# First eight attention blocks of an attention and expert kernel: order written by hand, fourth chunks' weights turned on TensorE

## The chip, the cores and the metric

One core of a Trainium2 chip runs the whole program. The metric is device time in microseconds. The core's engines are TensorE (PE in the profile, with its weight loads as PEld), VectorE (DVE), ScalarE (ACT), GpSimd (POOL) and SyncE (SP, which only issues DMAs here). Each runs its own list of instructions in the listed order and waits at an instruction until what it needs is there.

## What is computed

```python
# attention: q (4, 12288, 128), kv (4, 384, 32, 128), w_sr (128, 128)
kv_pool = kv.reshape(B, H // 4, 4, W // 4, 4, C).mean(axis=(2, 4))
k = v = kv_pool.reshape(B, -1, C) @ w_sr             # 768 keys for each batch
s = (q @ k.transpose(0, 2, 1)) / sqrt(C)
a = exp(s - s.max(-1)); a /= a.sum(-1) + 1e-9
x = (a @ v).reshape(B * N, C)                        # 49152 rows
# experts: w_gate (128, 8), w1 (8, 128, 1024), w2 (8, 1024, 128)
logits = x @ w_gate; e = argmax(logits); p = softmax(logits)[e]
y = p * (maximum(x @ w1[e], 0) @ w2[e])
```

## The kernel before

Rows go in 96 blocks of 512, 24 to a batch; a block has four chunks of 128 rows. Numbers are split in a high and a low half where needed (qh and ql, ah and its low half, xh and xl), so that a product is three matmuls.

**Keys of the first batch.** `kv_load` brings six tiles of raw keys in two halves each; `kv_pool` sums the first half on DVE (`pooled`), and `kv_turn` adds `pooled` and the eight pieces of the second half while turning them, nine matmuls in that order; `kv_turned` copies the result (`pT`), `kv_project` multiplies it with w_sr, `kv_high` and `kv_low` write the key halves `k_sb`.

**A block t of attention.** `q_load` (four DMAs), `q_turn` (DVE, qT), `q_high` (ACT, qh), `q_low` (ql). For each chunk c, `scores` is a generator in steps: six matmuls into a PSUM tile `s`; the row maximum `nmax` (DVE, lines 317 and 318); the exponentials `a` (ACT, line 321); the cast `ah`; the low half `ah` (POOL, line 332) and one DMA that turns both halves into `aT` (line 333). `block_values` multiplies aT with the values two blocks later (18 matmuls), `block_high` and `block_low` make xh and xl, `block_logits` and `block_sum` the gate's logits.

**Experts.** Blocks are grouped (two in the first group, then four); a group's gate (`gate`) finds its most frequent expert, `group_load` fetches that expert's weights, `weight_scales` and `split_expert` scale and split them. Block t - 8 goes through its expert while block t is at its scores (LAG is 8).

**What sets the order.** From block 8 on, a hand-written table of times (`at`, in steps of LEN = 18.7) sets the order of every engine; the times are only keys for sorting, nothing waits for them. The keys of the first batch and blocks 0 to 7 stand in a plain loop ahead of that (`early_scores`, `early_tick`, `early_values`), and the language's scheduler chooses the order on each engine from priorities. In these blocks the cast `ah` of every chunk is on DVE, ql is on DVE, and the DMAs of q are issued from ACT. PSUM holds two `s` tiles and a third (`s2`) for chunk 2, and two other banks (`ps_f`).

Where the text speaks of a step of the table, block t's step begins at t times 18.7, and the lines of that step are `block_scores` at +0, +3.65, +9.25 and +14.85, and `block_values` at +6.0 and +11.6.

## Time and profile before

| | |
|---|---|
| time, median of 3 runs | 1948.69 us (1944.15 to 1950.67) |
| profiled execution | 1945.67 us, of which the span is 1943.9 us |
| TensorE busy | 1877.9 us (97%), mean granted clock 0.989 of full speed |
| DVE, ACT, POOL busy | 1436.2, 1290.3, 1367.6 us |
| chain that ended last | PE 89%, DVE 4%, DMA 3% |

Times in rows are microseconds from the start of the span, unless marked ns. A duration of a matmul holds the way through the array, so matmuls overlap in the rows: the pace of TensorE is the distance between starts. PEclk is the granted clock of TensorE, 1.00 for 2.4 GHz and 0.50 for 1.2 GHz.

### The profile page before, as it was taken

Reading aid. Unit: us, or ns where it says so; the run is one execution under the profiler, and the core shown is the slowest. Engines: PE = TensorE matmul, PEld = TensorE weight load, DVE = VectorE, ACT = ScalarE, POOL = GpSimd, SP = SyncE. Lnnn points to the kernel's source line nnn. Section 1 sums busy time; section 2 is a strip of 40 time slices with the busy share of each in tenths; the row PEclk is TensorE's granted clock in tenths of the full one; section 3 lists DMA queues with packets and bytes.
Section 4 is the critical chain, followed back from the end, with each engine's and each line's share of the span. In section 5 each row is a group of like instructions: output and inputs, shape, how many; then the busy total and the mean of one; then the engine's idle time right before and its main releaser. Section 6 shows DMA issues by size and latency. Waiting matters only on the chain.

```text
span 1943.9 us, 30335 instructions
## 1 busy us (share of the span) xinstructions
PE 1877.9 (97%) x9908; PEld 1095.8 (56%) x9908; DVE 1436.2 (74%) x2800; ACT 1290.3 (66%) x2346; POOL 1367.6 (70%) x1385
## 2 busy tenths in 40 slices
PE   6779999999999999999999999999999999999987
PEld 5555555555555555555555555555555555555444
DVE  6787877778787787766777877867767667677685
ACT  2347667676767767767667667677677677676554
POOL 1567787776878777777688688677677776776353
PEclk9889999999999999999999999999999999999999
DMA  8798888767988876878888887776777777676352
GB/s 193 140 164 174 164 164 177 155 128 156 197 160 166 181 152 130 161 139 147 162 149 187 170 153 143 152 150 139 146 136 147 135 145 142 125 154 134 87 129 46
DMA packets 1012385, 290.61 MB, mean 149 GB/s; under 512 B 916960, under 2 KB 994914, under 8 KB 1012224
## 3 DMA queue, kind: packets, MB, share of 16 engines
q1 hardware_dynamic: 995072, 286.44, 74.5%
q10 hardware_dynamic: 16896, 2.10, 0.7%
q8 instruction: 79, 1.29, 0.3%
q14 instruction: 82, 0.67, 0.1%
q0 software_dynamic: 256, 0.10, 0.0%
HBM read 81.34 MB, written 30.15 MB: 57 GB/s over the span
## 4 chain that ended last, share of the span: by engine, by line
PE 89%; DVE 4%; DMA 3%; issue 1%; ACT 1%; POOL 0%; SPq 0%; ACTq 0%; POOLq 0%; DVEq 0%
PE m L136 44%; PE y L136 24%; PE s L136 21%; DMA aT<-ah 1%; DVE hl L454 1%; DVE nmax L317 1%; DMA kv_raw<-in_kv_dram 1%; DVE ah L326 1%; DMA aT<-in_kv_dram 0%; DVE ws L401 0%; ACT a L321 0%; ACT hh L448 0%; DMA q_sb<-in_q_dram 0%; ACT kv_raw L431 0%; SPq L178 0%
## 5 line engine op out<-in xcount | busy, mean ns | idle before, releaser
L332 POOL TENSOR_TENSOR ah<-a,ah 128x768 f16<-128x768 f32 x388 | 641.4, 1655 | 385.8 <-ACT ah L330 294.3
L448 ACT ACTIVATE hh<-m 128x512 f16<-128x512 f32 (+1 forms) x784 | 463.7, 593 | 411.3 <-PE m L136 408.2
L454 DVE SCALAR_TENSOR_TENSOR hl<-m,hh 128x512 f16<-128x512 f32 (+1 forms) x784 | 533.0, 681 | 228.2 <-ACT hh L448 199.0
L136 PE MATMUL s<-k_sb,qh 128*128 128x384 f32 x1552 | 476.9, 388 | 9.5 <-ACT qh L516 9.0
L321 ACT ACTIVATE a<-s,nmax 128x768 f32<-128x768 f32 x388 | 351.1, 905 | 167.1 <-DVE nmax L318 130.7
L136 PE MATMUL m<-aT,v_sb 128*128 128x512 f16 (+1 forms) x1764 | 413.1, 378 | 15.7 <-DMA aT<-ah 9.8
L317 DVE TENSOR_REDUCE nmax<-s 128x1 f32<-128x768 f32 x388 | 369.3, 953 | 73.2 <-PE s L136 64.9
L136 PEld LDWEIGHTS s<-k_sb,qh 128*128 128x128 f32 x1552 | 293.2, 193 | 68.0 <-ACT qh L516 10.2
L136 PE MATMUL m<-xh,w1h 128*128 128x512 f16 (+1 forms) x776 | 296.3, 382 | 7.5 <-DVE hl L454 6.7
L136 PE MATMUL y<-hh,w2h 128*128 128x512 f16 (+1 forms) x776 | 293.1, 378 | 2.7 <-ACT y L477 1.8
L136 PEld LDWEIGHTS <-v_sb 128*128 128x128 f16 x1764 | 170.9, 98 | 219.8 <-issue 11.7
L136 PE MATMUL m<-xl,w1h 128*128 128x512 f16 (+1 forms) x776 | 293.5, 378 | 0.0
L136 PE MATMUL y<-hh,w2l 128*128 128x512 f16 (+1 forms) x776 | 293.2, 378 | 0.0
L136 PE MATMUL m<-xh,w1l 128*128 128x512 f16 (+1 forms) x776 | 293.2, 378 | 0.0
L136 PE MATMUL y<-hl,w2h 128*128 128x512 f16 (+1 forms) x776 | 293.2, 378 | 0.0
L136 PE MATMUL s<-k_sb,ql 128*128 128x384 f32 x776 | 267.3, 345 | 2.5 <-DVE ql L521 2.4
L136 PEld LDWEIGHTS <-w2h 128*128 128x128 f16 x1552 | 151.6, 98 | 183.5 <-issue 6.2
L136 PEld LDWEIGHTS <-w1h 128*128 128x128 f16 x1552 | 125.0, 101 | 131.0 <-issue 56.2
L328 POOL CAST ah<-a 128x768 f16<-128x768 f32 x178 | 146.8, 824 | 72.2 <-ACT a L321 72.2
L348 DVE SCALAR_TENSOR_TENSOR xl<-m,xs,xh 128x512 f16<-128x512 f32 (+1 forms) x98 | 73.0, 745 | 130.7 <-ACT xh L343 128.6
L483 POOL COPY o<-yT 128x512 uint16<-128x512 uint16 x190 | 137.2, 767 | 22.8 <-DMA yT<-y 22.8
L330 ACT CAST ah<-a 128x768 f16<-128x768 f32 x178 | 148.9, 836 | 3.9 <-DMA aT<-ah 1.6
(211 smaller groups left out, 2037.4 us busy)
## 6 DMA issues: line engine op xcount, KB each, us to landing
kv_raw<-in_moe_w_dram SPq DMA_DIRECT2D x54, 512.0 KB, 4.7
out_dram<-o SPq DMA_DIRECT2D x96, 256.0 KB, 2.2
q_sb<-in_q_dram SPq DMA_DIRECT2D x352, 64.0 KB, 2.5
kv_raw<-in_kv_dram SPq DMA_DIRECT2D x84, 256.0 KB, 4.6
aT<-ah SPq DMA_TRANSPOSE x388, 3.8
aT<-in_kv_dram SPq DMA_DIRECT2D x12, 256.0 KB, 7.5
k_dram<-k_sb SPq DMA_DIRECT2D x8, 384.0 KB, 3.1
q_sb<-in_q_dram ACTq DMA_DIRECT2D x32, 64.0 KB, 3.0
```

The source lines that it names most:

```text
L136: nc.tensor.matmul(o, l, r, start=start, stop=stop)
L317: nc.vector.tensor_reduce(nmax, pss[:, :, :KH], axis=AX.XY, op=ALU.max, negate=True)
L321: nc.scalar.activation(a.rearrange("p (h k) -> p h k", h=2), pss[:, :, :KH], AF.Exp, bias=nmax, scale=1.0, accum_out=sums)
L326: nc.vector.tensor_copy(ah[:, 0], a)
L328: nc.gpsimd.tensor_copy(ah[:, 0], a)
L330: nc.scalar.copy(ah[:, 0], a)
L332: nc.gpsimd.tensor_sub(ah[:, 1], a, ah[:, 0])
L348: nc.vector.scalar_tensor_tensor(xl[:, :n], po[:, :n], k["xs"][:, 0:1], xh[:, :n], op0=ALU.mult, op1=ALU.subtract)
L448: nc.scalar.activation(hh[:, :n], ph[:, :n], AF.Relu)
L454: nc.vector.scalar_tensor_tensor(hl[:, :n], ph[:, :n], 0.0, hh[:, :n], op0=ALU.max, op1=ALU.subtract)
L483: nc.gpsimd.tensor_copy(o.bitcast(U16).rearrange("p c (d i) -> p i c d", i=2)[:, i], yT.rearrange("p (i c) d -> p i c d", i=2)[:, i])
```

## The change

The plain loop of blocks 0 to 7 is gone. `first_keys` and a new table, `plan_short`, write out their order by hand, in steps of SHORT = 9.8; `plan_first` places the first group's gate and its expert's weights in those steps, and `plan_group` has a case of its own for the second group. The table from block 8 on is as before. In the same go:

- `scores` has a second way for a chunk (`by_pe`), taken by chunk 3 of blocks 0 to 6: TensorE turns the exponentials `a` in six 128x128 transposes into two PSUM banks, ACT copies them to aT's high half (two copies of 128x384), DVE subtracts to the low half (two of 128x384). That chunk has no cast, no subtraction on POOL and no DMA.
- The casts of chunks 0 and 2 go from DVE to ACT and those of chunk 1 (and chunk 3 of block 7) to POOL, as they are from block 8 on; ql goes from DVE to POOL, except block 0's.
- PSUM is divided from the start as later: two `s` tiles, three banks m, one bank y. The third `s` tile goes; the values of blocks 0 to 5 go to bank y.
- q's DMAs of blocks 2 to 9 are issued from SP instead of ACT, behind the turning DMAs of the block before; q of block 0 is loaded in front of the last two tiles of keys.
- In a tile of keys the eight pieces of the second half are added first and `pooled` last.
- The four DMAs that keep the first batch's keys for the tail (`kv_keep`) go to the steps of blocks 11 to 14.

```diff
-    early = ExitStack()
-    ps_e = early.enter_context(tc.tile_pool(name="ps_e", bufs=1, space=bass.MemoryType.PSUM))
-    ps_f = early.enter_context(tc.tile_pool(name="ps_f", bufs=2, space=bass.MemoryType.PSUM))
-    EXPERTS = {}
+    EXPERTS = {name: sb.enter_context(tc.tile_pool(name=f"ps_{name}", bufs=1, space=bass.MemoryType.PSUM))
+               for name in "my"}
...
+        if by_pe:
+
+            kts = [slice(lo, lo + KT // 2) for lo in (0, KT // 2)]
+            pts = []
+            for ks in kts:
+                pt = bank()[:, :KH].rearrange("p (t c) -> p t c", c=P)
+                for i, t in enumerate(range(ks.start, ks.stop)):
+                    nc.tensor.transpose(pt[:, i], a[:, t * P:(t + 1) * P], ident)
+                pts.append(pt)
+            yield
+            for ks, pt in zip(kts, pts):
+                nc.scalar.copy(aT[:, ks, cs], pt)
+            yield
+            for ks, pt in zip(kts, pts):
+                nc.vector.tensor_sub(aT[:, KT + ks.start:KT + ks.stop, cs], pt, aT[:, ks, cs])
+            return
         ah = three.tile([P, 2, NK], F16, name="ah")
-        if not EXPERTS:
-            nc.vector.tensor_copy(ah[:, 0], a)
-        elif c % 2:
+        if c % 2:
             nc.gpsimd.tensor_copy(ah[:, 0], a)
         else:
             nc.scalar.copy(ah[:, 0], a)
...
-    raws = {t: kv_load(0, t) for t in range(KT)}
-    for t in range(2):
-        q_load(t, nc.sync)
+    raws = {}
+    for t in range(KT):
+        raws[t] = kv_load(0, t)
+        if t == KT - 3:
+            q_load(0, nc.sync)
+    q_load(1, nc.sync)
...
+    LEN, SHORT = 18.7, 9.8
+    FIRST = LAG * (LEN - SHORT)
...
+    def plan_short(t):
+
+        T, z, y = begin(t), t - 2, t - 3
+        by_pe = t < LAG - 1
+        for c, time in enumerate((0.0, 2.36, 4.72, 7.1)):
+            at(T + time, block_scores, t, c, by_pe and c == 3)
+            at(T + time + 1.1, block_part, t, c)
+            at(T + time + 2.3, block_part, t, c)
+        for c, times in enumerate(((5.76, 6.7), (5.8, 8.4), (8.1, 10.0))):
+            for time in times:
+                at(T + time, block_part, t, c)
...
+        if t > 0:
+            for time in (1.07, 3.42, 4.67):
+                at(T + time, block_part, t - 1, 3)
+        if z >= 0:
+            at(T + 3.43, block_values, z, range(0, 2))
+            at(T + 5.78, block_values, z, range(2, 4))
+            at(T + 8.16, block_values, z, range(4, KT))
+            at(T + SHORT + 0.8, block_high, z)
+            at(T + SHORT + 2.27, block_low, z)
...
+        at(T + 0.2, q_load, t + 2, nc.sync)
+        at(T + (-0.2 if t else 2.31), q_turn, t + 1)
+        at(T + (1.5 if t else 3.4), q_high, t + 1)
+        at(T + (1.95 if t else 3.4), q_low, t + 1, nc.gpsimd)
...
+        if t < LAG:
+
+            T = LAG * LEN
+            group_gate(g)
+            for _ in range(6):
+                at(T + 3.5, gate_part, g)
...
+        first_keys()
+        for t in range(LAG):
+            plan_short(t)
+            run(begin(t + 1) - 0.5)
```

From the end of block 8's step on, PE, DVE, ACT and POOL have the same instructions in the same order in both programs, and SP has too but for the four DMAs of `kv_keep`. What differs ahead of that is shown at three places.

TensorE at the end of the keys; m is the bank of a tile of keys, kv_raw its second half. Before:

```order
L136 MATMUL m<-ident,pooled 128x128
L136 MATMUL m<-ident,kv_raw 128x128 x8
L136 MATMUL m<-pT,wsr 128x128 x2
L136 MATMUL s<-k_sb,qh 128x384 x2
L136 MATMUL s<-k_sb,ql 128x384
```

Now:

```order
L131 MATMUL m_281<-ident,kv_raw 128x128 x8
L131 MATMUL m_290<-pT,wsr 128x128
L131 MATMUL m_281<-ident,pooled 128x128
L131 MATMUL m_299<-pT,wsr 128x128
L131 MATMUL s<-k_sb,qh 128x384 x2
L131 MATMUL s<-k_sb,ql 128x384
```

The eight pieces of the last tile and the projection of the tile before now stand in front of `pooled`.

VectorE in the step of block 3. Before:

```order
L326 CAST ah<-a 128x768
L512 STREAM_TRANSPOSE qT<-q_sb 128x512
L326 CAST ah<-a 128x768
L521 TENSOR_TENSOR ql<-qT,qh 128x512
L317 TENSOR_REDUCE nmax<-s 128x1
L348 SCALAR_TENSOR_TENSOR xl<-m,xs,xh 128x512
L318 TENSOR_SCALAR nmax<-nmax 128x1
L326 CAST ah<-a 128x768
L317 TENSOR_REDUCE nmax<-s 128x1
L326 CAST ah<-a 128x768
L318 TENSOR_SCALAR nmax<-nmax 128x1
L317 TENSOR_REDUCE nmax<-s 128x1
```

Now:

```order
L309 TENSOR_REDUCE nmax<-s 128x1
L310 TENSOR_SCALAR nmax<-nmax 128x1
L354 SCALAR_TENSOR_TENSOR xl<-y,xs,xh 128x512
L309 TENSOR_REDUCE nmax<-s 128x1
L310 TENSOR_SCALAR nmax<-nmax 128x1
L367 TENSOR_REDUCE lg<-m_639 128x32
L330 TENSOR_TENSOR aT<-m_613,aT 128x3x128
L330 TENSOR_TENSOR aT<-m_617,aT 128x3x128
L309 TENSOR_REDUCE nmax<-s 128x1
L310 TENSOR_SCALAR nmax<-nmax 128x1
L309 TENSOR_REDUCE nmax<-s 128x1
L310 TENSOR_SCALAR nmax<-nmax 128x1
```

The four casts and ql have left; the two subtractions of the fourth chunk of the block before have come, and each nmax has its line 310 right behind it.

ScalarE in the same step. Before:

```order
L321 ACTIVATE a,sums<-s_645,nmax 128x768
L343 ACTIVATE xh<-m,xs 128x512
L508 DMA q_sb<-in_q_dram 32x16x32
L321 ACTIVATE a,sums<-s,nmax 128x768
L508 DMA q_sb<-in_q_dram 32x16x32 x3
L321 ACTIVATE a,sums<-s,nmax 128x768 x2
L516 CAST qh<-qT 128x512
```

Now:

```order
L313 ACTIVATE a,sums<-s,nmax 128x768
L327 CAST aT<-m_613 128x3x128
L327 CAST aT<-m_617 128x3x128
L313 ACTIVATE a,sums<-s,nmax 128x768
L336 CAST ah<-a 128x768
L313 ACTIVATE a,sums<-s,nmax 128x768
L336 CAST ah<-a 128x768
L313 ACTIVATE a,sums<-s,nmax 128x768
L349 ACTIVATE xh<-y,xs 128x512
L522 CAST qh<-qT 128x512
```

The four issues of q have left ScalarE; two copies and two casts have come between the exponentials.

## Rows read from the trace of the kernel before

**Rows 1.** Windows: us, busy us (count) of each engine, PEclk, DMA share, GB/s.

```profile
32.60:143.90 111.30, 82.63 (x384) 58.03 (x385) 89.60 (x179) 44.68 (x87) 63.90 (x46) 0.85 0.82 153
...
181.34:368.50 187.16, 187.16 (x994) 108.75 (x992) 143.66 (x258) 129.06 (x240) 150.40 (x160) 1.00 0.84 167
```

**Rows 2.** Waits, 32.5 to 144: waiter, awaited, us in total, times, longest.

```profile
PE m L136 <- DMA aT<-ah: 9.8, 3, 3.7
...
PE s L136 <- ACT qh L516: 9.0, 5, 3.8
```

**Rows 3.** Groups by form, 32.6 to 143.9: busy us, mean ns, idle before.

```profile
L332 POOL TENSOR_TENSOR ah<-a,ah 128x768 f16<-128x768 f32 x32 | 55.9, 1747 | 71.6 <-DVE ah L326 55.4 <-issue 5.9 <-DVE gate L373 3.0
...
L317 DVE TENSOR_REDUCE nmax<-s 128x1 f32<-128x768 f32 x33 | 30.8, 950 | 16.0 <-PE s L136 16.0
...
L321 ACT ACTIVATE a<-s,nmax 128x768 f32<-128x768 f32 x33 | 29.8, 902 | 59.1 <-DVE nmax L318 39.6 <-DVE vst L239 3.8 <-DVE nmax L317 3.5
...
L326 DVE CAST ah<-a 128x768 f16<-128x768 f32 x32 | 27.3, 854 | 3.3 <-DMA aT<-ah 3.1
...
L521 DVE TENSOR_TENSOR ql<-qT,qh 128x512 fp32r<-128x512 f32 x9 | 6.9, 766 | 1.4 <-ACT qh L516 1.4
```

**Rows 4.** Timeline of TensorE, first step of the later table: start, us, instruction.

```profile
132.01 0.62 PE L136 MATMUL s<-k_sb,qh 128*128 128x384 f32 x2 [1.24 <-ACT qh L516]
...
143.86 2.10 PE L136 MATMUL m<-aT,v_sb 128*128 128x512 f16 x9 [0.60 <-DVE hl L454]
...
152.50 0.69 PE L136 MATMUL s<-k_sb,qh 128*128 128x384 f32 x2
```

**Rows 5.** Timeline, end of the keys.

```profile
26.36 1.89 DVE L186 TENSOR_REDUCE pooled<-kv_raw 128x128 f32<-128x1024 f32 x1 [1.64 <-DMA kv_raw<-in_kv_dram]
...
30.50 0.71 DVE L512 STREAM_TRANSPOSE qT<-q_sb 128x512 f32<-128x512 f32 x1 [1.86 <-DMA q_sb<-in_q_dram]
```

**Rows 6.** The same of TensorE.

```profile
28.70 1.95 PE L136 MATMUL m<-ident,kv_raw 128*128 128x128 f32 x16
...
32.60 0.62 PE L136 MATMUL s<-k_sb,qh 128*128 128x384 f32 x2 [1.04 <-ACT qh L516]
```

**Rows 7.** DMA queues and issues, 32.6 to 143.9: packets, MB, share; KB, us to landing.

```profile
q1 hardware_dynamic: 53323, 14.87, 69.8%
q10 hardware_dynamic: 16896, 2.10, 12.0%
...
q_sb<-in_q_dram ACTq DMA_DIRECT2D x31, 64.0 KB, 3.0
...
aT<-ah SPq DMA_TRANSPOSE x32, 4.1
```

**Rows 8.** Timeline of TensorE in a later step, with transposes of 128x128 f32.

```profile
763.12 0.52 PE L136 MATMUL s<-k_sb,qh 128*128 128x384 f32 x2
...
763.66 0.38 PE L272 MATMUL s<-ident,vT 128*128 128x128 f32 x2
763.88 0.38 PE L136 MATMUL m<-xh,w1h 128*128 128x512 f16 x1
```

**Rows 9.** Groups by form, 400 to 1500, as rows 3.

```profile
L454 DVE SCALAR_TENSOR_TENSOR hl<-m,hh 128x512 f16<-128x512 f32 x466 | 319.9, 687 | 135.1 <-ACT hh L448 116.2
...
L330 ACT CAST ah<-a 128x768 f16<-128x768 f32 x116 | 97.1, 837 | 2.7 <-DMA aT<-ah 1.6
L328 POOL CAST ah<-a 128x768 f16<-128x768 f32 x116 | 95.6, 824 | 47.4 <-ACT a L321 47.4
...
L521 POOL TENSOR_TENSOR ql<-qT,qh 128x512 fp32r<-128x512 f32 x58 | 73.7, 1270 | 4.6 <-ACT qh L516 4.5
...
L431 ACT ACTIVATE kv_raw<-kv_raw,ws 128x1024 f32<-128x1024 f32 x31 | 35.6, 1149 | 0.5
```

**Rows 10.** Windows of 1 us, columns as rows 1.

```profile
41.00:42.00 1.00, 0.43 (x2) 0.43 (x3) 1.00 (x2) 0.00 (x0) 1.00 (x1) 1.00 0.14 29
...
43.00:44.00 1.00, 0.99 (x4) 0.48 (x2) 1.00 (x4) 0.37 (x1) 0.50 (x2) 0.50 0.80 150
```

More of the change, by code (lines that the diff above doesn't have):

```diff
@@ L198, in kv_turn @@
         k["pt"] = pt
-        parts = [k.pop(("pooled", t))] + k.pop(("parts", t), [])
+        parts = k.pop(("parts", t), []) + [k.pop(("pooled", t))]
         if len(parts) == 1:
@@ L557, in block_values @@
             if kt == 0:
-                BL[t]["po"] = bank(start, end)
+                BL[t]["po"] = bank(start, end) if start else EXPERTS["y"].tile([P, 512], F32, name="y")
             values(BL[t]["po"], BL[t]["aT"], k, kt, BLK)
@@ L877, in done, with first_keys @@
         return 0 <= t < NBLK
-    raws = {t: kv_load(0, t) for t in range(KT)}
-    for t in range(2):
-        q_load(t, nc.sync)
-    gate_weights()
-    def kv_project_all(b, t):
-        kv_project(b, t, bank()[:, :P])
-        kv_high(b, t)
-        kv_low(b, t)
-    for t in range(KT):
-        kv_pool(0, t, raws.pop(t))
-        kv_turn(0, t, bank()[:, :P])
-        kv_turned(0, t)
-        if t == KT - 1:
-            q_prep(0)
-        if t > 0:
-            kv_project_all(0, t - 1)
-    kv_project_all(0, KT - 1)
+    raws = {}
[4 more added lines that the diff above has]
+    q_load(1, nc.sync)
+    gate_weights()
+    def first_keys():
+        for t in range(KT):
+            kv_pool(0, t, raws.pop(t))
+            pt = bank()[:, :P]
+            k = KEYS[0]
+            own = k.pop(("pooled", t))
+            parts = k.pop(("parts", t))
+            for i, part_ in enumerate(parts):
+                mm(pt, part_, ident, i == 0, False)
+            if t > 0:
+                kv_project(0, t - 1, bank()[:, :P])
+                kv_high(0, t - 1)
+            mm(pt, own, ident, False, True)
+            k["pt"] = pt
+            kv_turned(0, t)
+            if t > 0:
+                kv_low(0, t - 1)
+            if t == KT - 2:
+                q_prep(0)
+        kv_project(0, KT - 1, bank()[:, :P])
+        kv_high(0, KT - 1)
+        kv_low(0, KT - 1)
     extra = [dict(n=TAIL) for _ in range(EXTRA)] if tail else []
@@ L907, in closes @@
         return GRP[t] if done(t) and t == GROUPS[GRP[t]][-1] else None
[L909 to L925 removed]
     def early_values(t, lo, hi):
         if done(t):
[L929 removed]
+            block_values(t, range(lo, hi), 1)
             if hi == KT:
@@ new lines, in plan_short @@
+    def plan_short(t):
[8 more added lines that the diff above has]
+                at(T + time, block_part, t, c)
+        if not by_pe:
+            at(T + 11.7, block_part, t, 3)
+            at(T + 12.5, block_part, t, 3)
+        if t > 0:
+            for time in (1.07, 3.42, 4.67):
[6 more added lines that the diff above has]
+            at(T + SHORT + 2.27, block_low, z)
+            if t < LAG - 1:
+                at(T + SHORT + 3.41, lambda: block_logits(z, bank()))
+                at(T + SHORT + 4.62, block_sum, z)
+        at(T + 0.2, q_load, t + 2, nc.sync)
+        at(T + (-0.2 if t else 2.31), q_turn, t + 1)
+        at(T + (1.5 if t else 3.4), q_high, t + 1)
+        at(T + (1.95 if t else 3.4), q_low, t + 1, nc.gpsimd)
+        if t == 0:
+            at(T + 3.47, kv_scale, 0)
+            beside(0, 3, kv_spread, 0)
+            at(T + 9.4, kv_units, 0)
+            at(T + 9.4, kv_units_rest, 0)
+        if t == 1:
+            for time, t0, n in ((3.43, 0, 4), (5.78, 4, KT - 4)):
+                at(T + time, lambda t0=t0, n=n: kv_values(0, t0, n, bank().rearrange("p (t c) -> p t c", c=P)))
+                at(T + time + 0.9, kv_values_high, 0, t0, n)
+                at(T + time + 1.3, kv_values_low, 0, t0, n)
+        if closes(y) is not None:
+            plan_first(t)
@@ new lines, in plan_group @@
+    def plan_group(g, t):
+        if t < LAG:
+            T = LAG * LEN
+            group_gate(g)
+            for _ in range(6):
+                at(T + 3.5, gate_part, g)
+            at(T + 6.1, group_count, g)
+            beside(LAG, 2, group_votes, g)
+            at(T + 11.4, group_first, g)
+            at(T + 11.45, group_load, g)
+            at(T + 12.35, gate_part, g)
+            at(T + 12.4, group_left, g)
+            at(T + 15.0, gate_part, g)
+            return plan_weights(g, t + 1)
```

115 lines of the change are left out of this document (43 added, 72 removed).

## Prediction

> **What bounds the kernel now.** I looked first at the stretches of time, to see where TensorE is not busy. From about 144 on it is busy all the time at the full clock, as the second row of windows shows [rows 1], and the steps there are 18.72 long (187.16 for ten). So whatever brings that stretch forward by a microsecond brings the end forward by one, as long as TensorE stays busy, and its instructions there are the same in both programs. The stretch of the first eight blocks, 32.60 to 143.90, is another matter: TensorE is busy for 82.63 of 111.30 and has a mean clock of 0.85, so part of that busy time runs at half speed. The waits say on what: 9.8 in three waits for a turning DMA and 9.0 in five for qh [rows 2]. Behind both stands VectorE, which is busy for 89.60 [rows 1]: POOL waits 55.4 for its casts before it can subtract and hand over to that DMA, and ACT waits 39.6 for nmax [rows 3]. A cast on DVE costs 0.854 in the mean, 27.3 in all, and stands between one nmax and the next. So the stretch is bound by DVE's list, which is both long and badly placed, and no engine is full.
>
> To have one point to compare, I take the place where the later table's step 8 would have begun had it run at its steady pace from the start: chunk 3's scores stand at +14.85 of the step and began at 152.50, so it is 137.65 [rows 4]. Its first scores really began at 132.01; the 5.64 between were lost in going over. From the first scores at 32.60 [rows 6] to 137.65 it is 105.05, and the change is worth what it takes off that and off the keys.
>
> **The keys.** q of block 0 now comes in front of the last eight of the 24 key DMAs. The price of a q tile: ACT's queue carried 33 of these DMAs of 64 KB (2.10 MB) and took 12.0% of 111.3, 13.4, so four cost 1.62 of all sixteen DMA engines [rows 7]. The last tile's first half, which let DVE sum at 26.36 [rows 5], then lands at 28.0, and `pooled` is there at 29.9. The second half had landed by 28.70, since its eight pieces began then without a wait of their own [rows 6]; now it lands between 28.0 and 30.3. The pieces take 1.95 and no longer wait for `pooled`, so they end between 30.0 and 32.3, and `pooled` and its copy and projection follow (about 1.2, an estimate from a piece's 0.24 and two handovers). What goes is q's late landing: DVE waited for it until 30.50 [rows 5], and the first scores waited for qh until 32.60. First scores then between 31.2 and 33.5; I take 32.1, since the second half follows the first in the same queue at once. Worth 0.5.
>
> **Eight blocks.** For each engine I work out what a block holds.
>
> TensorE, by distances between starts at the full clock: three score matmuls from 763.12 to 763.66, 0.18 each, two transposes in 0.22 [rows 8], nine value matmuls in 2.10 of which the last 0.38 is the way through [rows 4, 8], 0.215 each. So 24 x 0.18 = 4.32, 18 x 0.215 = 3.87, six transposes 0.66, and some 0.2 for eight short gate matmuls: 9.05.
>
> DVE: 89.60, less the casts 27.3 and eight of the nine ql at 0.766 (6.1) [rows 1, 3], plus 14 subtractions of 128x384 from PSUM. None stands in the trace; hl with 512 columns takes 0.687 [rows 9], half a 768-column cast 0.42, so 0.42 to 0.69, and I take 0.55, the nearer to hl in kind: 7.7. That is 63.9, 8.0 a block.
>
> ACT: 44.68 plus 16 casts at 0.837 (13.4) [rows 1, 9] plus 14 copies at 0.42 to 0.69, taken at 0.5 (7.0): 65.1, 8.1 a block. Also its 31 issues of q go [rows 7].
>
> POOL: 63.90, less seven subtractions at 1.747 (12.2), plus nine casts at 0.824 (7.4) and eight ql at 1.27 (10.2) [rows 1, 3, 9]: 69.3, 8.7 a block.
>
> DMA: the other queue took 69.8% of 111.3, 77.7, with 32 turning DMAs and some stores and weights [rows 7], so at most 2.43 a turning DMA. Three and a q tile are at most 8.9.
>
> So every sum lies below TensorE's 9.05, if closely. Since values are multiplied two blocks later, a turning DMA with its 4.1 to landing [rows 7] has a whole block in hand, and the long waits for it should go. What is left are short waits around the two `s` tiles (a third one goes). A tile is held for its six matmuls (1.1), nmax (0.95) and a (0.90) with the small instructions between, some 3.6, and two tiles must give four chunks in 9.05, 4.5 for each: about 0.9 of play, which a 0.84 cast on ACT or a 0.7 instruction on DVE ahead of a row maximum can just use up.
>
> Blocks 0 and 1 have no values; there the tiles set the pace, at least 7.2, and block 0 has the scaling of the keys on DVE in between. I take 8.8 each. For blocks 2 to 5 I take 9.65, 0.6 over TensorE's sum, for the first group's gate on DVE in blocks 4 and 5 and the like. In blocks 6 and 7 ACT has the four large activations of the expert's weights, 1.149 each [rows 9]. They are in the 65.1; without them a block is 7.6 and with two of them 9.9: 10.0 each. Sum: 17.6 + 38.6 + 20.0 = 76.2. The low end, no waits at all from block 2 on, is 17.6 + 54.3 = 71.9. As high end I take blocks of 11.4, halfway between 9.05 and today's 13.9 (111.3 by 8): 91.
>
> **Going over.** Today this costs 5.64 [rows 4]. The six gate parts of the second group still stand in a row on DVE there, but without casts between and with TensorE's first expert matmuls ready. I take 1.0, from 0 to 5.6.
>
> **Sum.** 32.1 + 76.2 + 1.0 = 109.3 against 137.65: 28.3 earlier. The profiled execution took 1945.67, so 1917.3; the median of the runs lies 3.0 above it, by which it would be 1920.3. I say 1919.0. By the low ends (31.2 + 71.9) it is 34.6, 1911; by the high ends (33.5 + 91 + 3) it is 10.2, 1935. The steps of blocks 11 to 14 take over four stores on SP, which are off TensorE's path: nothing. A measurement of this kernel can tell about 0.3% from no change, 5.8, so the line for faster is 1942.8.
>
> **Rivals.** First, *q late behind SP*. The four issues of q for block t + 2 now wait on SP behind chunk 2's turning DMA, which waits for POOL's subtraction, and the next q_turn stands on DVE ahead of the next row maximum. By the table the subtraction ends at 1.9 of the step, q is issued by 5.3 and landed by 8.3 (3.0 to landing [rows 7]) while q_turn stands at 9.6: 1.3 to spare. If the DMA queues, at up to 8.9 of 9.05, make landings two or three longer, or POOL at 8.7 falls behind, every block from 2 on loses some 2: 12 to 16 over the forecast, 1931 to 1935. For it speaks how full both are; against it that ACT's issues were delayed alike. Chance 0.15.
>
> Second, *the clock*. TensorE now falls to half speed after short waits: in the window from 41 it is busy for 0.43, and in the one from 43, after matmuls in small bursts, it has 0.50 [rows 10]. The blocks to come have such short waits at every chunk, and blocks 0 and 1 leave TensorE half idle. At 1.2 GHz a block's TensorE work is 18.1, and six such blocks are 109 in place of 58.6: 50 later, 1969, slower than before. It decides from 13 a block on (105 by 8), which is nearly half the time at the lower clock. Against it: an engine at half speed has twice the busy share and leaves no gaps, and the full clock came back each time once TensorE was kept busy. Chance 0.03. The Trainium skill speaks for this rival (TensorE: Matmul & The Clock Gate, "A second HAM failure mode: psum-queue depth-cycling"): short idle times while cycling through PSUM banks can make the clock swing between its two levels. The trace agrees in kind (0.85 over the stretch [rows 1]). By that rule the stretch would keep a mean clock like today's 0.85, and by it alone the blocks from 2 on would be 10.6 instead of 9.65, some 6 later.
>
> Third, *nothing comes of it*: the step after block 8 waits for something other than TensorE, such as the second group's weights, and gives the gain back, about 1946. Against it stands that this part of the table is the same and TensorE had no wait there. Chance 0.05.
>
> Fourth, *no waits at all*: 1911. Chance 0.1.
>
> **Chances.** The forecast (1914 to 1926) has 0.67. Range 1910 to 1935, with the clock, the rival of no gain and some of the tails outside. Faster by over 0.3%: 0.67 + 0.15 + 0.1 = 0.92; within: 0.05; slower: 0.03.
>
> **What would show it.** In the profile after: first scores at 32.1; TensorE about 95% busy at a clock near 1.00 from block 2 on; scores of successive blocks 9.65 apart; no wait over 1 for a turning DMA; the later steps still 18.72; chunk 3 of block 8's step at 124.2 (109.3 + 14.85). Blocks 11 apart with DVE waiting for q would be the first rival, a PEclk of 0.5 in blocks 2 to 5 the second, and steps over 18.72 behind block 8 the third.

## The result, and the profile of the changed kernel

| | before | after |
|---|---|---|
| time, median of 4 runs | 1949.46 us (1944.15 to 1950.67) | 1927.97 us (1925.31 to 1929.67) |
| profiled execution (span) | 1945.67 (1943.9) us | 1929.05 (1927.3) us |
| TensorE busy, mean granted clock | 1877.9 us, 0.989 | 1875.2 us, 0.994 |

The ratio is 0.9894, with a 95% interval from 0.9871 to 0.9916: faster by 21.5 us. The forecast said 1919.0, most likely 1914 to 1926, in a range from 1910 to 1935: the result lies in the range, 2 above the likely part. The sum said 28.3 earlier. First the stretches, in the columns of [rows 1]: blocks 0 and 1, blocks 2 to 7, and ten later steps.

```profile
34.82:53.88 19.06, 14.53 (x64) 12.21 (x63) 15.03 (x35) 12.12 (x26) 10.43 (x8) 0.82 0.45 76
53.88:114.74 60.86, 56.10 (x332) 39.80 (x333) 46.53 (x102) 48.00 (x89) 45.42 (x37) 1.00 0.90 161
...
181.34:368.50 187.16, 187.16 (x997) 109.29 (x995) 145.82 (x268) 128.61 (x245) 144.21 (x149) 1.00 0.87 172
```

The eight blocks take 79.92 (34.82 to 114.74), where before it was 111.30 with the way into the later table [rows 1]. In blocks 2 to 7 TensorE is busy for 92% at the full clock; ten later steps take 187.16 as before. What TensorE still waits for, from the first scores to the step behind block 8:

```profile
PE s L131 <- ACT a L313: 4.5, 6, 1.3
PE m L323 <- ACT a L313: 3.1, 5, 0.9
PE m L131 <- DVE lg L367: 2.3, 1, 2.3
PE m L131 <- DVE xl L354: 2.2, 4, 1.0
PE m L131 <- DVE hl L460: 1.5, 1, 1.5
```

TensorE's waits for a turning DMA and for qh of [rows 2], 18.8 together, are gone (POOL still waits for a turning DMA three times ahead of a cast, 3.2 at the longest). The groups of these eight blocks (34.82 to 114.74) beside [rows 3]:

```profile
L338 POOL TENSOR_TENSOR ah<-a,ah 128x768 f16<-128x768 f32 x22 | 35.8, 1650 | 2.3 <-ACT ah L336 2.1
...
L313 ACT ACTIVATE a<-s,nmax 128x768 f32<-128x768 f32 x31 | 28.0, 903 | 14.7 <-DVE nmax L310 12.2 <-PE s L131 1.7 <-POOL ah L338 0.3
...
L330 DVE TENSOR_TENSOR aT<-m,aT 128x384 f16<-128x384 f32 x14 | 7.1, 549 | 0.1
...
L327 ACT CAST aT<-m 128x384 f16<-128x384 f32 x14 | 5.9, 480 | 0.0
```

ScalarE waited 39.6 for nmax and waits 12.2. POOL's 71.6 ahead of its subtractions [rows 3] can't be set beside the 2.3 as it stands. Before, and now:

```profile
POOL ah L332 <- DVE ah L326: 55.4, 15, 37.2
```

```profile
POOL ql L527 <- ACT qh L522: 42.5, 4, 37.8
```

The longest wait in each is POOL's idle time from 1.6 us on to its first work of these blocks (at 38.85 before, at 39.39 now), which now stands in front of a ql. Without it POOL waited 34.4 ahead of its subtractions and waits 2.3 now, with 12.3 ahead of its casts and 4.7 ahead of ql.

**Against the forecast's sum.** The point of comparison (start of chunk 3's scores in block 8's step, less 14.85) is 130.52 - 14.85 = 115.67; the forecast said 109.3, before it was 137.65 [rows 4].

| term | forecast | measured | difference |
|---|---|---|---|
| first scores | 32.1 | 34.82 | 2.7 late |
| eight blocks | 76.2 | 79.92 | 3.7 late |
| going over | 1.0 | 0.93 | none |
| the step after | nothing lost | one wait of 2.33 | 2.3 late |

So 28.3 less 2.7, 3.7 and 2.3 leaves 19.6 at the steps behind, and chunk for chunk the later blocks stand 18.8 to 21.0 earlier than before. (The profiled executions are only 16.6 apart: between 111 and 42 us before the end this one took 4 longer than before, with the same instructions. The granted clock is 0.50 from 1857 to 1864 here and 1.00 in that part before; all twelve experiments have a stretch at 0.50 there too. What brings it on, no run shows.) The experiments take the three losses in turn, then what carried the gain.

The head of the program, VectorE and then TensorE, after:

```profile
29.34 0.29 DVE L224 SCALAR_TENSOR_TENSOR k_sb<-m,k_sb 128x128 fp32r<-128x128 f32 x1 [3.63 <-ACT vT L219]
...
29.73 0.70 DVE L518 STREAM_TRANSPOSE qT<-q_sb 128x512 f32<-128x512 f32 x1
...
31.73 1.88 DVE L181 TENSOR_REDUCE pooled<-kv_raw 128x128 f32<-128x1024 f32 x1
```

```profile
25.93 2.47 PE L131 MATMUL m<-ident,aT 128*128 128x128 f32 x16 [3.79 <-DMA aT<-in_kv_dram]
...
33.66 0.49 PE L131 MATMUL m<-ident,pooled 128*128 128x128 f32 x2 [1.44 <-DVE pooled L181]
...
34.82 0.60 PE L131 MATMUL s<-k_sb,qh 128*128 128x384 f32 x2
```

The last sum started at 31.73 and not at 28.0: VectorE stood for 3.63 at the low half of tile 3 (`k_sb`), which needs that tile's projection, which TensorE has behind the pieces of tile 4, which came at 25.93. Then q's turn and ql went first as well. A part of the 3.63 is the clock: those pieces took 2.47, and 1.95 for as many before [rows 6], since the granted clock fell in them (0.93 from 24 to 28 and 0.65 from 28 to 32, where it was 1.00 before).

### The profile page after: what moved, and what is told of

Same layout as the page of the kernel before. It is cut to its first block, busy times and chain, and to the rows that moved or that the text cites. A ratio compares the mean times of both kernels' runs of the same rounds, so it can differ in the third digit from the quotient of the medians.

```text
span 1927.3 us, 30394 instructions
## 1 busy us (share of the span) xinstructions
PE 1875.2 (97%) x9950; PEld 1095.0 (57%) x9950; DVE 1419.7 (74%) x2774; ACT 1306.2 (68%) x2376; POOL 1365.6 (71%) x1395
## 4 chain that ended last, share of the span: by engine, by line
PE 88%; DVE 4%; DMA 3%; issue 2%; POOL 1%; ACT 1%; SPq 1%; POOLq 0%; DVEq 0%; ACTq 0%
PE m L131 44%; PE y L131 25%; PE s L131 20%; DVE hl L460 1%; DMA aT<-ah 1%; DMA kv_raw<-in_kv_dram 1%; POOL ah L338 1%; SPq L173 0%; DMA aT<-in_kv_dram 0%; DVE nmax L309 0%; ACT a L313 0%; ACT hh L454 0%; DVE ws L407 0%; DMA kv_raw<-in_moe_w_dram 0%; DMA yT<-y 0%
## 5 line engine op out<-in xcount | busy, mean ns | idle before, releaser
L338 POOL TENSOR_TENSOR ah<-a,ah 128x768 f16<-128x768 f32 x381 | 626.0, 1647 | 313.0 <-ACT ah L336 297.8
L131 PE MATMUL s<-k_sb,qh 128*128 128x384 f32 x1552 | 469.9, 383 | 4.7 <-ACT a L313 4.5
L131 PE MATMUL m<-aT,v_sb 128*128 128x512 f16 (+1 forms) x1656 | 383.6, 377 | 1.6 <-DVE hl L460 1.6
L131 PEld LDWEIGHTS s<-k_sb,qh 128*128 128x128 f32 x1552 | 288.0, 190 | 61.7 <-ACT a L313 6.7
L131 PE MATMUL s<-k_sb,ql 128*128 128x384 f32 x776 | 262.8, 339 | 0.6 <-DVE ql L295 0.6
L334 POOL CAST ah<-a 128x768 f16<-128x768 f32 x187 | 154.3, 825 | 85.6 <-ACT a L313 80.7
L336 ACT CAST ah<-a 128x768 f16<-128x768 f32 x194 | 161.9, 834 | 9.5 <-issue 3.6
L354 DVE SCALAR_TENSOR_TENSOR xl<-m,xs,xh 128x512 f16<-128x512 f32 (+1 forms) x92 | 68.6, 745 | 129.2 <-ACT xh L349 127.3
L527 POOL TENSOR_TENSOR ql<-qT,qh 128x512 fp32r<-128x512 f32 x95 | 120.9, 1272 | 48.5 <-ACT qh L522 48.3
```

The costliest lines, as they stand in the source:

```text
L131: nc.tensor.matmul(o, l, r, start=start, stop=stop)
L334: nc.gpsimd.tensor_copy(ah[:, 0], a)
L336: nc.scalar.copy(ah[:, 0], a)
L338: nc.gpsimd.tensor_sub(ah[:, 1], a, ah[:, 0])
L354: nc.vector.scalar_tensor_tensor(xl[:, :n], po[:, :n], k["xs"][:, 0:1], xh[:, :n], op0=ALU.mult, op1=ALU.subtract)
L527: by.tensor_sub(ql, BL[t].pop("qT"), qh)
```

## Experiments

A time without a note is that of a single run; after took 1927.97 in the median.

### The head: q in front of the last keys, and the ring

**e1**, q behind all keys and its turn behind the last sum:

```diff
-        if t == KT - 3:
-            q_load(0, nc.sync)
+    q_load(0, nc.sync)
...
+            if t == KT - 1:
+                q_prep(0)
...
-            if t == KT - 2:
-                q_prep(0)
```

> The changed kernel with q of block 0 loaded behind all keys, as before the change, and with block 0's q_turn, q_high and q_low behind the sum of the last tile of keys on VectorE instead of ahead of it. In the changed kernel the first scores begin at 34.82. Theory 'order on VectorE': that sum stood behind q's three instructions, and these behind the low half of tile 3's keys, which had to wait for the eight pieces of tile 4; q's place in the DMA queue matters little, so this run and the one with the order alone (e2) begin their scores within 0.5 of each other, at 32.2 to 33.2. Theory 'late keys': q in front of the last tiles holds them up, the last sum begins at 26.4 here as before the change, and the first scores come at 31.9 to 32.4, at least 1 earlier than in e2. From the first scores to the scores of block 8 it should be 79.9 as in the changed kernel.

**e2**, q's turn behind the last sum only (the second and third part of that diff):

> The changed kernel, with q of block 0 in front of the last two tiles as changed; alone the order on VectorE differs: block 0's q_turn and q_low stand behind the sum of the last tile of keys. Theory 'order on VectorE': the sum, which began at 31.73 in the changed kernel, begins when its keys land, before 29.7, and the first scores at 32.4 to 33.2 instead of 34.82; the whole run is some 2 shorter. Theory 'late keys': the keys land late, the sum begins no earlier than 31, and the first scores come no earlier than 34.3.

e1: 1922.72, first scores at 27.72, below everything expected. e2: 1928.56, the last sum at 30.05 and first scores at 34.03, which fits neither theory. Moving q's turn alone is worth 0.8; the sum then stood behind the low half of tile 3, which had waited 3.83. (That the kernel took no less time than after has its cause behind block 8, see there.) In e1:

```profile
22.90 1.91 DVE L181 TENSOR_REDUCE pooled<-kv_raw 128x128 f32<-128x1024 f32 x1
25.55 0.71 DVE L518 STREAM_TRANSPOSE qT<-q_sb 128x512 f32<-128x512 f32 x1 [0.74 <-DMA q_sb<-in_q_dram]
```

The last sum started 8.8 earlier than in after. Part of that is no effect of the edit. Windows of 4 us, the last number is GB/s; before, after, and e1:

```profile
8.00:12.00 4.00, 3.79 (x18) 3.64 (x18) 1.41 (x5) 0.00 (x0) 0.00 (x0) 1.00 1.04 261
...
16.00:20.00 4.00, 2.25 (x18) 2.08 (x18) 2.11 (x2) 0.28 (x1) 0.00 (x0) 1.00 1.06 279
```

```profile
8.00:12.00 4.00, 3.86 (x18) 3.89 (x18) 1.29 (x5) 0.00 (x0) 0.00 (x0) 1.00 1.06 270
...
16.00:20.00 4.00, 2.83 (x23) 2.62 (x24) 3.27 (x5) 0.65 (x3) 0.00 (x0) 1.00 1.14 239
20.00:24.00 4.00, 2.14 (x20) 1.95 (x18) 1.62 (x4) 0.61 (x3) 0.00 (x0) 1.00 0.80 225
```

```profile
8.00:12.00 4.00, 4.00 (x23) 4.00 (x23) 2.09 (x5) 0.28 (x1) 0.00 (x0) 1.00 1.03 370
...
16.00:20.00 4.00, 3.09 (x24) 2.88 (x25) 3.27 (x7) 1.32 (x6) 0.00 (x0) 1.00 1.06 343
```

From 8 to 12 all three load the same keys (q's first issue in after is at 13.94), and the rate is 261, 270 and 370 GB/s: it differs by execution (e2, run beside e1 on the same chip, had 259). What the edit does is seen behind 16: with q in front the rate falls to 239 and 225, with q behind it holds (279 and 343). By windows of 1 us it is 158 in after from 19 to 20 and 50 from 20 to 21, at a DMA share of 0.33: the queue had nearly run empty. SP had spent 3.66 on the four issues of q (from 13.94), as long as on the four of keys ahead of them (3.55), which bring four times the bytes.

**e5**, e1 with the sum added first and the pieces after it, as in the kernel before:

```diff
+            mm(pt, own, ident, True, False)
             for i, part_ in enumerate(parts):
-                mm(pt, part_, ident, i == 0, False)
+                mm(pt, part_, ident, False, i == len(parts) - 1)
...
-            mm(pt, own, ident, False, True)
...
```

> As e1 (q behind all keys, its turn behind the last sum), but in a tile of keys the sum pooled is added first again and the eight pieces after it, as in the kernel before. I read the interval from the start of the last pooled sum on VectorE to the first scores, since the landing of the keys itself differs between executions (260 to 390 GB/s). In e1 it was 4.82. Theory 'order of the pieces': the 1.95 of the pieces come behind the sum's end and the interval becomes 6.0 to 6.4 (before: 6.24). Rival 'q decides': q landed 2.65 behind the start of that sum, and the chain q_turn, qh, scores from there takes the same as in e1, so 4.8 to 5.2. Second question, how fast keys land with q behind them: theory 'q in front drains the queue': no gap in the memory rate ahead of the last key piece, and the last pooled starts at 22.5 to 26.5 as in e1 (22.90) and before (26.36). Theory 'e1 had a lucky execution and q is no matter': it starts at 28 to 32 as in after (31.73, behind q's turn) and e2 (30.05).

1939.56, first scores at 42.20, 6.88 behind the last sum's start: later than either theory gave, and the last sum itself only at 35.32, though the rate was 278 to 292 GB/s and no q was in front. VectorE shows why:

```profile
28.07 0.29 DVE L224 SCALAR_TENSOR_TENSOR k_sb<-m,k_sb 128x128 fp32r<-128x128 f32 x1 [4.60 <-ACT vT L219]
...
34.92 0.29 DVE L224 SCALAR_TENSOR_TENSOR k_sb<-m,k_sb 128x128 fp32r<-128x128 f32 x1 [4.58 <-ACT vT L219]
...
35.32 1.86 DVE L181 TENSOR_REDUCE pooled<-kv_raw 128x128 f32<-128x1024 f32 x1
```

The hand-written order is a ring: the sum of a tile stands behind the low half of the tile two before, that behind a projection, that behind the pieces of the tile between, and here these again behind a sum. Each tile then takes 5.3 (from 16.30 to 21.62) to 6.9, whatever the DMAs do. The longer ones are those where the granted clock fell (0.65 from 24 to 28) and the pieces took 3.2 for 1.95; the 6.88 behind the last sum has that in it too. Adding the pieces first opens the ring. What stays is its other half: a sum still stands behind the low half of the tile two before, and that behind the pieces of the tile between. That is what held the last sum in after.

**e12** tests that directly; q stays in front:

```diff
+        kv_pool(0, 0, raws.pop(0))
         for t in range(KT):
-            kv_pool(0, t, raws.pop(t))
...
             kv_turned(0, t)
+            if t < KT - 1:
+                kv_pool(0, t + 1, raws.pop(t + 1))
             if t > 0:
                 kv_low(0, t - 1)
```

> As after (q of block 0 still in front of the last two tiles of keys), but on VectorE the sum pooled of the next tile stands ahead of the low half of the tile before, not behind it. Theory 'a ring in the hand-written order': in after the last sum waited until 31.73, though its rows had landed by about 28, since VectorE stood at the low half of tile 3, which waits for that tile's projection, which stands on TensorE behind the pieces of tile 4. Then the last sum starts at 27 to 29 and the first scores come at 31.5 to 33.0, near the 32.1 of the forecast, against 34.82, 34.03, 33.38, 34.38 and 33.4 in the five runs so far with q in front. Rival 'the landing alone': first scores stay at 33.4 to 34.8, since the last pieces land too late for anything else to matter. Later steps then earlier than in after by as much as the first scores, 1926 to 1927 for the first theory.

```profile
28.67 1.91 DVE L181 TENSOR_REDUCE pooled<-kv_raw 128x128 f32<-128x1024 f32 x1 [2.39 <-DMA kv_raw<-in_kv_dram]
```

The last sum now waits for its rows alone and starts at 28.67, first scores come at 33.05 (0.05 above the expected range), and the kernel took 1925.72; the later steps are 0.8 to 2.0 earlier than in after. So this order on VectorE cost up to 1.8 of the 2.7, 3.1 at the sum. And the price of q in front can be read at the sum: before, at 261 to 279 GB/s, these rows had come at 26.36 [rows 5]; here, at 266 to 275 ahead of q, at 28.67: 2.3, where the forecast had 1.62. e9 (below) has the head of e1, q behind all keys, at 267 to 284 GB/s:

```profile
26.22 1.89 DVE L181 TENSOR_REDUCE pooled<-kv_raw 128x128 f32<-128x1024 f32 x1
29.66 0.71 DVE L518 STREAM_TRANSPOSE qT<-q_sb 128x512 f32<-128x512 f32 x1 [1.56 <-DMA q_sb<-in_q_dram]
```

Its sum is as early as before, but its first scores, at 31.84, then wait for q. So at the first scores q in front costs some 1.2 (33.05 against 31.84), not 2.3; each of these is one execution.

### The step behind block 8

**e3**, the second group's weight maxima and what follows them later:

```diff
-            return plan_weights(g, t + 1)
+            return plan_weights(g, t + 1, True)
...
-        at(T + 17.1, scales_part, g)
+        at(T + (LEN + 2.5 if late else 17.1), scales_part, g)
         T += LEN
-        at(T + 0.7, scales_part, g)
-        beside(t + 1, 1, scales_part, g)
-        at(T + 5.8, scales_part, g)
+        at(T + (4.2 if late else 0.7), scales_part, g)
+        beside(t + 1, 2 if late else 1, scales_part, g)
+        at(T + (10.5 if late else 5.8), scales_part, g)
...
-        at(T + 9.25, split_part, g, 0)
+        at(T + (12.0 if late else 9.25), split_part, g, 0)
```

> The changed kernel with the two maxima over the second group's expert weights moved on VectorE from the end of block 8's step and the start of block 9's into block 9's step (behind the low halves of hidden parts 0 and 1), the matmul on them to chunk 2 and what follows behind it by 2.7 to 4.7. In the changed kernel VectorE waits 2.31 for the weights' DMA there, and TensorE behind it 2.33. Theory 'weights come late': that wait goes, and block 9's second half and all later steps come 2.0 to 2.5 earlier against the changed kernel. Rival: the wait is only handed on, TensorE waits in block 10's step for the split weights, and nothing is gained (within 0.5).

In after, VectorE and TensorE stood like this:

```profile
136.12 1.22 DVE L407 TENSOR_REDUCE ws<-kv_raw 128x1 f32<-128x1024 f32 x1 [2.31 <-DMA kv_raw<-in_moe_w_dram]
...
137.85 0.21 DVE L367 TENSOR_REDUCE lg<-m 128x32 f32<-128x64 f32 x1
```

```profile
138.11 0.38 PE L131 MATMUL m<-xh,w1h 128*128 128x512 f16 x1 [2.33 <-DVE lg L367]
```

The maximum of the weights (`ws`) waits for their DMA, which the change had put 4.35 later in that step (11.45 for 7.1), the logits stand behind it, and TensorE behind these. In e3 the wait is gone from TensorE's list. Beside after, e3 stands 0.83 earlier at `xh` of block 6 and 3.14 at that of block 8, so the wait is worth 2.3, as expected; the kernel took 1924.79.

The same wait could cost more than its length. In after the clock stayed at 1.00 behind it. In e2, e10 and e5 it was 3.34, 2.78 and 3.01, and the granted clock fell behind it; in e2:

```profile
138.00:140.00 2.00, 1.41 (x4) 0.55 (x4) 2.00 (x4) 0.00 (x0) 0.00 (x0) 0.55 1.10 204
```

There the later steps of these three lost 2.1 to 2.5 more than those of after. So e2 stood 0.5 ahead of after at block 6's `xh` and 2.0 behind it at block 7's, and e10 (below) lost more than its eight blocks did.

### What the eight blocks are made of

**e11**, the 25 casts that are left in them back on VectorE:

```diff
-        if c % 2:
+        if early:
+            nc.vector.tensor_copy(ah[:, 0], a)
+        elif c % 2:
```

> As after, but the 25 casts that are left in the first eight blocks stand on VectorE as before, instead of 16 on ScalarE and 9 on GpSimd; the hand-written order and the fourth chunks on TensorE stay. Theory 'VectorE's list bound these blocks': 25 by 0.854 are 21.4, VectorE's work per block goes from 7.8 to 10.4, so blocks of 10.4 at the least, the eight in 87 to 95 and the kernel 7 to 15 slower than after. Rival 'the order alone made the gain': VectorE had 24% idle in these blocks in after, casts fit in there, and the eight blocks stay within 80 to 83.

1942.01; the eight blocks take 94.24 (33.08 to 127.32), 14.3 more than in after.

```profile
33.08:127.32 94.24, 74.83 (x396) 55.45 (x396) 74.53 (x159) 48.28 (x98) 51.85 (x37) 0.89 0.63 119
```

```profile
ACT a L313 <- DVE nmax L310: 39.4, 23, 3.8
```

VectorE's 74.53 are 79% of the stretch: as a sum the casts would have fitted, for VectorE had 18.4 idle in after and they hold it for 17.4. ScalarE again waits 39.4 for nmax, 39.6 before [rows 3]. So the sum does not set the price; ScalarE's wait speaks for the place of a cast, between one row maximum and the next.

The mean of 0.854 for a cast [rows 3] also hides two kinds. Casts that started with POOL idle took 0.52 to 0.56. Those that started while POOL was at a subtraction ended 0.41 to 0.42 behind its end, as here in the kernel before (78.59 and 79.00), and took up to 1.61 in these blocks; the exceptions began in the last 0.1 of one:

```profile
76.95 1.64 POOL L332 TENSOR_TENSOR ah<-a,ah 128x768 f16<-128x768 f32 x1 [2.14 <-DVE ah L326]
77.41 1.59 DVE L326 CAST ah<-a 128x768 f16<-128x768 f32 x1
```

In e11 it is the same (0.55, and up to 1.34). So a part of what the casts cost on VectorE is time in which they stood until POOL was done, and a sum by engine counts that as work.

**e4**, the fourth chunks by DMA like the others (`by_pe = False`):

> The changed kernel without the turning on TensorE: chunk 3 of all eight blocks goes over POOL (cast and subtraction) and a turning DMA, everything else of the order by hand stays. Theory 'POOL and the DMA queues could not carry four chunks': POOL then holds 8.7 + 2.5 x 7/8 = 10.8 a block and the DMA queues some 10.4, so the eight blocks take 86 to 92 from the first scores to block 8's, not 79.9, and the run is 6 to 12 longer. Rival 'the order alone did it': blocks stay at 10, and since TensorE no longer waits for chunk 3's exponentials (3.1 in five waits) the eight blocks are the same or some 3 shorter.

1940.74; the eight blocks take 89.7 (34.38 to 124.12), 9.8 more.

```profile
34.38:124.12 89.74, 72.50 (x355) 51.20 (x354) 57.16 (x122) 53.62 (x99) 71.40 (x57) 0.89 0.87 153
```

```profile
PE s L131 <- ACT a L313: 14.7, 10, 3.6
```

```profile
ACT ah L336 <- DMA aT<-ah: 5.4, 2, 4.3
```

POOL has 71.40 where it has 55.85 in after, and TensorE waits 14.7 for exponentials. One link of that chain is the third row (waits of ScalarE): a cast waits for a turning DMA, 4.3 at the longest, with the next exponentials behind it. In e11 and e4 the mean clock of the stretch is 0.89, in after 0.96: some of the 14.3 and the 9.8 is time at half speed.

**e10**, q's DMAs issued from ScalarE's queue as before (`q_load` with `nc.scalar` in `plan_short`):

> As after, but q of blocks 2 to 9 is issued from ScalarE's queue as before, not from SP behind the turning DMAs. Theory 'q is in time on SP' (in after VectorE waited for q once, 1.2): the eight blocks stay at 79.4 to 80.5, or take up to 1 more since ScalarE spends time on the 32 issues. Rival 'q late behind SP' (the forecast's first rival): VectorE's wait goes and the blocks become 1 to 2 shorter in sum or more.

Neither: 1936.74, the eight blocks 85.33 (34.42 to 119.75), 5.4 more than in after. ScalarE's timeline of one block, with its queue's issues (ACTq):

```profile
55.50 1.36 ACTq L514 DMA_DIRECT2D q_sb<-in_q_dram  x2
...
56.91 1.83 ACTq L514 DMA_DIRECT2D q_sb<-in_q_dram  x2
58.78 0.62 ACT L522 CAST qh<-qT 128x512 fp32r<-128x512 f32 x1 [2.39 <-issue]
```

Four issues hold the queue from 55.50 to 58.74, and ScalarE's next instruction starts behind them; none of that counts as busy. The Trainium skill (Trainium Kernel Development and Optimization, "Key Constraints") says that spreading DMA issues over several engines saves only the sequencer's issue time; the trace agrees that this time is what matters, here 3.2 of this block's 11.07, on the engine that makes the exponentials. In the eight blocks four issues took 1.9 to 3.2.

The prices of e11, e4 and e10 (14.3, 9.8 and 5.4) add up to 29.5, more than the 24.2 that the change took off this stretch (105.05 to 80.85, with the going over). They overlap, and none is a share of the gain. What the order by hand, ql on POOL and the new division of PSUM give by themselves, no run shows.

**e6**, transposes and logits later in a short step, and the first group's vote too:

```diff
-            for time in (1.07, 3.42, 4.67):
+            for time in (2.4, 4.7, 5.95):
...
-                at(T + SHORT + 3.41, lambda: block_logits(z, bank()))
-                at(T + SHORT + 4.62, block_sum, z)
+                at(T + SHORT + 4.7, lambda: block_logits(z, bank()))
+                at(T + SHORT + 5.9, block_sum, z)
...
-            at(T + 4.64, gate_part, g)
-        at(T + 4.66, group_count, g)
+            at(T + 5.92, gate_part, g)
+        at(T + 5.94, group_count, g)
...
-        at(T + 9.4, group_first, g)
+        at(T + 10.95, group_first, g)
```

> In the short steps the six transposes of the fourth chunk stand behind chunk 1's scores instead of ahead of them, their copies and subtractions behind chunk 2's, the gate's logits behind the first third of the values (4.7 instead of 3.41 of the step), and the first group's vote is read behind the next block's first row maximum. All else as in after. Theory 'waits by order on TensorE' (0.9 for exponentials in front of the transposes and 0.3 to 1.0 for xl in front of the logits in most blocks make up the 3.7 that the eight blocks took over the forecast): the eight blocks go from 79.9 to 76.5 to 78.5, no wait for xl over 0.3. Rival 'two s tiles set the pace': chunk 1's scores need the same exponentials that the transposes need, so the waits only change their name, and the eight blocks stay at 79 to 80.5.

1936.07, the eight blocks 91.2 (33.39 to 124.59). The edit made waits of its own:

```profile
PE s L131 <- DVE votes L592: 4.3, 1, 4.3
...
PE s L131 <- DVE votes L606: 2.1, 1, 2.1
```

The count of the votes came too late for its matmul, an `s` tile was held until the vote was read, and a bank m was late (1.9). So this run says nothing on the question. **e8** has the same order on top of e7 (below):

> e7 with the order of e6 in the short steps. Theory 'waits by order on TensorE': the eight blocks in 76.5 to 78.5 and 1.5 to 3 less than e7: 1916 to 1920. Rival 'two s tiles set the pace': blocks 79 to 80.5 in all and the time of e7 within 1, 1919 to 1922. Either way faster than the changed kernel by 5 or more if q in front of the keys and the weights' wait are what cost it.

1934.30 in the median (ratio to before 0.9920, 0.9907 to 0.9934), with the waits of 4.3 and 2.1 again and the eight blocks in 90.6. **e9** mends the order: the vote and its logits as in after, block 0's transposes too, the vote read behind q's turn:

```diff
+            for time in (1.07, 3.42, 4.67) if t == 1 else (2.4, 4.7, 5.95):
...
+                w = 0 if t == 3 else 1.29
+                at(T + SHORT + 3.41 + w, lambda: block_logits(z, bank()))
+                at(T + SHORT + 4.62 + w, block_sum, z)
...
+        at(T + 9.65, group_first, g)
```

> e7 with the order of e8, but where e8 lost: the vote of the first group and its logits stay at their old places, and so do block 0's transposes, which took the banks of the scaled keys. The vote is read behind the turning of the next q instead of ahead of it. Theory 'order on TensorE' (e8's blocks 2 to 4 took 8.66, 9.42 and 9.43 against e7's 9.36, 9.94 and 10.00, and its loss came from votes 4.3 and 2.1 and a bank 1.8): blocks 2 to 7 are 0.5 shorter each, the eight blocks 76.5 to 78.5 against 80.2 in e7, and the median 1919 to 1921.5. Rival 'two s tiles set the pace': the gain of those blocks is given back in the blocks with the vote and the weights, the eight blocks stay at 79.5 to 80.5 and the median at 1922 to 1924.

(The 8.66 quoted there was misread: e8's blocks 2 and 3 took 10.31 and 9.43.) Median 1923.99 (ratio 0.9881, 0.9861 to 0.9901); the eight blocks take 81.49 (31.84 to 113.33), 80.17 in e7. Blocks 2 to 5 did become shorter, 39.61 against 40.40. TensorE's waits in the eight blocks, e9:

```profile
PE s L131 <- ACT a L313: 9.1, 10, 1.9
```

and e7:

```profile
PE s L131 <- ACT a L313: 4.2, 6, 1.6
PE m L323 <- ACT a L313: 3.4, 6, 0.8
```

The wait of the transposes became one of the scores, as the rival said: both need the same exponentials, and 9.1 stands where 7.6 stood, with 1.9 of it in block 6. That block took 13.08, 10.57 in e7. There a cast on ScalarE waited for a turning DMA ahead of the exponentials, TensorE waited 1.93 for these, and the windows of 2 us show what came then:

```profile
92.04 0.83 ACT L336 CAST ah<-a 128x768 f16<-128x768 f32 x1 [2.59 <-DMA aT<-ah]
```

```profile
94.00:96.00 2.00, 2.00 (x13) 2.00 (x14) 1.97 (x4) 1.30 (x3) 1.35 (x2) 0.81 1.12 206
96.00:98.00 2.00, 2.00 (x7) 0.88 (x6) 1.86 (x9) 1.21 (x3) 0.52 (x1) 0.50 1.14 209
```

The granted clock fell to 0.50, 1.2 GHz, and six value matmuls took 2.60 instead of 1.47. So the wait cost twice. The mended order is no gain in this run; with block 6 lost that way, it doesn't settle whether it could be one.

### Both mends together

**e7** is e1 and e3 in one:

> e1 and e3 together: q behind all keys with its turn behind the last sum, and the second group's weight maxima in the step after. Theory 'terms add, q in front costs 3 to 6': first scores at 27.5 to 31, no wait of 2.3 in the step after block 8, 1919 to 1922 in the median (1927.97 less 2.3 less 4 to 7). Rival 'e1 had fast memory by chance': first scores at 31 to 34 and 1923 to 1926.

Median 1922.71 of four runs (1920.68 to 1924.45), ratio to before 0.9869 (0.9853 to 0.9884), and each run lies below every run of both kernels: 5.3 below the changed one by the medians (which was not run beside it, and the intervals of the two ratios overlap a little). First scores at 29.88 at 297 to 330 GB/s, no wait of 2.3 behind block 8. The median lies 0.7 above its expected range. First scores with q behind the keys came at 27.72, 29.88, 30.41 and 31.84 (e1, e7, e8, e9; not e5, with its ring), with q in front at 33.05 to 34.82 (after, e2, e3, e4, e6, e10, e11, e12); e3 and e8 had about the same rate ahead of q, 297 to 305 and 288 to 311, and are 3.0 apart, q's turn included.

## Why the prediction was right, and where it was not

**What bound the kernel**: right. Between the keys and the tail TensorE fell idle in the first eight blocks alone, the steps behind moved by what those gained, less one wait, and stayed at 18.72. e11 shows the other half, that the casts on VectorE were badly placed: put back, they cost 14.3. One reading was off: of the 55.4 that POOL was said to wait for casts, 37.2 is its idle time ahead of its first subtraction, and 18.2 is left. That the result lies in the range is not luck by errors that cancelled: all three losses went the same way.

**The keys**: wrong in sign. The forecast gained 0.5 and the change lost 2.2 (34.82 against 32.60 [rows 6]). Two steps failed. q in front makes the last sum's rows 2.3 late, not 1.62 (1.2 are left of it at the first scores): a share of the queue's busy time was taken for the price, but the rate also fell with q's DMAs of 64 KB and behind them (239 and 225 GB/s, 50 for 1 us). And the step that the last tile's first half lands at 28.0 and `pooled` is there at 29.9 took it that VectorE would be free. The order of the instructions, not the landing, decided: 31.73 in after, 28.67 in e12. This path can be read from the two orders without a run; I followed the last tile and not the one before.

**Engine sums**: good, and on the safe side. Measured per block (windows by 8): VectorE 7.7 for 8.0, ScalarE 7.5 for 8.1, POOL 7.0 for 8.7 (three of its 25 subtractions fall behind this window). The new subtraction took 0.549 (taken 0.55), the copy 0.480 (0.5). For six transposes the row says 0.87 with the way through, in line with 0.11 for each [rows 8].

**Eight blocks**: 79.92 for 76.2, the term most under-sized. They took 9.22, 9.84, 9.36, 10.05, 10.12, 11.07, 10.59 and 9.67. Most of the 3.7 is in block 1 (1.0 over), block 5 (1.4, where the vote stands on VectorE ahead of q's turn and a row maximum) and blocks 0, 3, 4 and 6 (0.4 to 0.6); blocks 2 and 7 were 0.3 under. In block 5 VectorE stood like this:

```profile
85.15 0.17 DVE L601 TENSOR_REDUCE votes<-s 128x1 f32<-128x8 f32 x1 [1.82 <-ACT a L313]
...
86.65 0.92 DVE L309 TENSOR_REDUCE nmax<-s 128x1 f32<-128x768 f32 x1
```

TensorE's rows are short waits: up to 0.9 for exponentials in front of the transposes, 1.0 for xl in front of the logits. The forecast found 0.9 of play in the two tiles s, said that a single instruction can use it up, and then took 0.6 for everything of the kind. So the term that was sized too small is this one: 0.6 a block was taken for the waits, and blocks 3 to 6 needed 1.0 to 2.0 over TensorE's 9.05. That the tiles set this rather than the order on TensorE is argued and not shown: in e9, with the order changed, the waits for exponentials did not shrink, but its blocks 2 to 5 got 0.8 shorter, and no run gives a third tile back.

**q's issues off ScalarE**: the prediction counted them ("also its 31 issues of q go") and gave them no price. e10 prices them at 5.4 in this order. So a part of the gain credited to the casts may have been this one.

**Going over**: right, 0.93 for 1.0. But the wait moved one step on: 2.33 for the second group's weights. The third rival had named that mechanism, against it stood "this part of the table is the same"; its load, though, had moved from 7.1 to 11.45, which the diff shows.

**The rivals.** *q late behind SP* was not seen: VectorE waited once, 1.2, for q. *The clock* hardly in after: 0.82 in blocks 0 and 1, 1.00 from block 2 on. The Trainium skill (TensorE: Matmul & The Clock Gate, "A second HAM failure mode: psum-queue depth-cycling") would have short idle times make the clock swing. In after no row shows it from block 2 on, with nine waits up to 1.0 in blocks 2 to 7. In e9 the clock did fall after a wait of 1.93, in e2, e10 and e5 behind block 8, and e4 and e11, with waits of up to 3.6 and 2.2 in these blocks, have 0.89 in the mean. So the rival's mechanism is there, and the change had little of it. *No waits at all* did not come.

## What to carry to other kernels

In a hand-written order, follow each instruction's inputs back over the queues for one whole turn of the loop: if the path comes back to the same queue, the turn has a price of its own, and the order of two additions can decide it. Give DMA issues on a computing engine a duration like any instruction, since they don't count as busy and stand between those that matter. When a chunk waits for exponentials, moving other work past the wait can merely rename it, as in e9. A wait counted from the start of a program belongs to no stretch: look at its longest part before two totals are compared.
